# Linear-attention and ReGLU block on one core: PSUM banks by least recent use, split load queues, stages interleaved across phases

## The chip, the cores and the metric

The kernel runs on one core of a Trainium2 chip. The metric is device time in microseconds (us) of one execution. Single executions of one kernel mostly agree within 0.3%. A profile is one execution; its span (first to last instruction) is about 1.7 us shorter than its time.

Engines: PE is TensorE, DVE is VectorE, ACT is ScalarE, POOL is GpSimd, SP issues most loads and stores. PSUM is the memory that matmuls write to: 8 banks of 128 x 512 float32.

## The reference, cut to what matters

One token block of S = 2048 rows, D = 1024, F = 3584, 32 heads of 32, all bfloat16:

```python
h  = x + linear_attention(layernorm(x), wqkv, wo)   # phi(t) = where(t > 0, t + 1, exp(t)) + 1e-6
h2 = h + W_down( relu(LN(h) @ W_gate) * (LN(h) @ W_up) )
# attention per head: kv = phi(k)^T v ; z = sum phi(k) ; o = phi(q) kv / (phi(q) z + 1e-6)
```

A "tile" below is 128 rows; there are 16. The stages are: projections of k and v (KV, 64 groups of 8 matmuls), q (Q, 32 groups), phi(k)^T v (KVACC), then per tile numerator and denominator (ND), output projection with residual (A) and the second layer norm (LN2), then the feed-forward part: gate/up (GU) and down (DN) in four chunks of 512 rows.

## The kernel before

A small Python scheduler records each engine's instructions in the order of the program text. Each engine runs its own list strictly in that order; waits on semaphores are derived from buffers. This is the middle stage:

```python
for i in range(NT + 3):
    if i < NT:
        ND(i)                                   # PE: 8 matmuls into banks 5,6,7
                                                # DVE: 3 denominators, reciprocal, 3 multiplies -> otile
    if 0 <= i - 1 < NT:
        transpose_tile(otile ... i - 1)         # PE 8 transposes, ACT evacuates
    if 0 <= i - 2 < NT:
        A(i - 2, 0); A(i - 2, 1)                # PE 2 x 8 matmuls, DVE adds the residual into xh
        LN2(i - 2)                              # DVE bn_stats x2, aggregate, eps; POOL pow; DVE; ACT normalises
    if 0 <= i - 3 < NT:
        transpose_tile(ln2tile ... i - 3)       # PE, ACT
```

All 32 Q groups come before this loop and all GU groups after it. At the start, the loads of x and of the weights alternate on one queue; tile after tile is normalised on DVE, transposed, and multiplied with all four 512-column blocks of the k and v weights:

```python
load_x(0, 1); load_wkv(0); load_x(1, 1); load_wkv(1); ...
LN1(0); LN1(1); transpose 0; transpose 1
for t in range(NT):
    LN1(t + 2)
    for j in range(4): KV(t, j)
    transpose(t + 2)
```

Of the kernel before, what the change touches and what calls it, by code (L numbers as in the profile page):

```python
# [9 lines left out]
P = 128  # L10
# [11 lines left out]
class Buf:  # L22
    __slots__ = ("name", "writers", "readers", "exclusive")

    def __init__(self, name, exclusive=False):
        self.name = name
        self.writers = []
        self.readers = []
        self.exclusive = exclusive

# [30 lines left out]
class Sched:  # L61
# [38 lines left out]
    def _deps(self, eng, reads, writes, extra):  # L100
        deps = list(extra)
        semnum = eng.sem.num if eng.sem is not None else -1
        for b in reads:
            deps += b.deps_for_read(semnum)
        for b in writes:
            deps += b.deps_for_write()
        return deps
# [74 lines left out]
def bass_sequential_preLN__linear_attn_block__glu_gated_reglu__prompt_kernel(  # L182
# [21 lines left out]
    NS = 5  # L204
    NDB = (NG + 2) // 3
    EPS_LN = 1e-5

# [12 lines left out]
    WQ = al(PK + NT * D)  # L220
    SLOTS = X0
    slot_sz = al(KT * FPS * P)
    firstpart = max(WQ + KT * D - X0, NS * 2 * slot_sz)
    VEXT = al(X0 + firstpart)
    OT = VEXT
    vext_sz = NT * NG * 129
    Y0 = al(VEXT + max(vext_sz, KT * S))
    LN1TILES = Y0
    OTILES = Y0
    PHITMP = al(Y0 + 2 * D)  # L230
    LN2TILES = PHITMP
    CONSTS = al(PHITMP + max(4 * 512, 2 * D))
# [3 lines left out]
    WO = al(MASK4 + 4)  # L236
    KVZ = al(WO + KT * D)
    END1 = al(KVZ + NG * 132)
    WD = al(X0 + NS * 2 * slot_sz)
# [5 lines left out]
    with ExitStack() as es:  # L245
# [10 lines left out]
        stats2 = sbf("stats2", [P, NT, DC, 6])  # L256
        mv2 = sbf("mv2", [P, NT, 2])
# [34 lines left out]
        oT = view(OT, KT * S).rearrange("p (k s) -> p k s", k=KT)  # L292
        ln1tile = [view(LN1TILES + i * D, D) for i in range(2)]
        otile = [view(OTILES + i * D, D) for i in range(2)]
        etmp = [view(PHITMP + i * 512, 512) for i in range(2)]
        ttmp = [view(PHITMP + (2 + i) * 512, 512) for i in range(2)]
        ln2tile = [view(LN2TILES + i * D, D) for i in range(2)]
# [15 lines left out]

        b_x = [[Buf(f"x{t}_{n}") for n in range(DC)] for t in range(NT)]
        b_ln1T = [Buf(f"ln1T{t}") for t in range(NT)]
        b_ln2T = [Buf(f"ln2T{t}") for t in range(NT)]
        b_wkv = [Buf(f"wkv{j}") for j in range(2 * DC)]
        b_wq = [Buf(f"wq{j}") for j in range(DC)]
# [5 lines left out]
        b_hh = [Buf(f"hh{f}") for f in range(FT)]  # L324
        b_slot_g = [Buf(f"slotg{i}") for i in range(NS)]
        b_slot_u = [Buf(f"slotu{i}") for i in range(NS)]
        b_oT = [Buf(f"oT{t}") for t in range(NT)]
        b_ln1tile = [Buf(f"ln1tile{i}") for i in range(2)]
        b_otile = [Buf(f"otile{i}") for i in range(2)]
        b_etmp = [Buf(f"etmp{i}") for i in range(2)]  # L330
        b_ttmp = [Buf(f"ttmp{i}") for i in range(2)]
        b_ln2tile = [Buf(f"ln2tile{i}") for i in range(2)]
# [3 lines left out]
        b_kvz = [Buf(f"kvz{g}") for g in range(NG)]  # L336
        b_wd = [Buf(f"wd{i}") for i in range(4)]
        b_relu = [Buf(f"relu{i}") for i in range(2)]
        b_stage = [Buf(f"stage{i}") for i in range(4)]
        b_ps = [Buf(f"psum{i}", exclusive=True) for i in range(8)]  # L340
        b_stats1 = [Buf(f"stats1_{t}") for t in range(NT)]
        b_mv1 = [Buf(f"mv1_{t}") for t in range(NT)]
        b_veps1 = [Buf(f"veps1_{t}") for t in range(NT)]
        b_rstd1 = [Buf(f"rstd1_{t}") for t in range(NT)]
        b_stats2 = [Buf(f"stats2_{t}") for t in range(NT)]
        b_mv2 = [Buf(f"mv2_{t}") for t in range(NT)]
        b_veps2 = [Buf(f"veps2_{t}") for t in range(NT)]
        b_rstd2 = [Buf(f"rstd2_{t}") for t in range(NT)]
        b_nmr2 = [Buf(f"nmr2_{t}") for t in range(NT)]
        b_mhalf = Buf("mhalf")  # L350
        b_deneps = [Buf(f"deneps{i}") for i in range(2)]
        b_rden = [Buf(f"rden{i}") for i in range(2)]

        E = Sd.emit

        E("pool", lambda e: e.memset(ident, 1.0), writes=[b_ident])
        E("pool", lambda e: e.affine_select(ident, ident, pattern=[[-1, P]], compare_op=ALU.is_equal, fill=0.0,
                                            base=0, channel_multiplier=1), reads=[b_ident], writes=[b_ident])
        E("pool", lambda e: e.memset(mhalf[:], -0.5), writes=[b_mhalf])
# [7 lines left out]
        def load_x(t0, m):  # L367
            s_ = dsem()
            src = x2[t0 * P:(t0 + m) * P, :].rearrange("(t p) d -> p t d", p=P)
            Sd.dma("sp", lambda e: e.dma_start(xh[:, t0:t0 + m, :], src), s_,  # L370
                   writes=[b for t in range(t0, t0 + m) for b in b_x[t]])

        def load_wkv(j):
            s_ = dsem()
            src = A_wqkv[:, D + j * 512:D + (j + 1) * 512].rearrange("(k p) n -> p k n", p=P)
            Sd.dma("sp", lambda e: e.dma_start(wkv[:, :, j * 512:(j + 1) * 512], src), s_, writes=[b_wkv[j]])

        def load_wq(j):
            s_ = dsem()
            src = A_wqkv[:, j * 512:(j + 1) * 512].rearrange("(k p) n -> p k n", p=P)  # L380
            Sd.dma("sp", lambda e: e.dma_start(wq[:, :, j * 512:(j + 1) * 512], src), s_, writes=[b_wq[j]])

        def load_wo():
            s_ = dsem()
            src = A_wo.rearrange("(k p) n -> p k n", p=P)
            Sd.dma("sp", lambda e: e.dma_start(wo, src), s_, writes=[b_wo])

        load_x(0, 1)
        load_wkv(0)
        if NT > 1:  # L390
            load_x(1, 1)
        load_wkv(1)
        t0 = 2
        while t0 < NT:
# [3 lines left out]
            if t0 == 4:  # L398
                for j in range(2, 2 * DC):
                    load_wkv(j)  # L400
        if NT <= 4:
            for j in range(2, 2 * DC):
                load_wkv(j)
        for j in range(DC):
            load_wq(j)
        load_wo()

        psT_ring = Ring([0, 1])
        acc_ring = Ring([2, 3, 4, 5, 6, 7])
        phi_ring = Ring([0, 1])  # L410

        def LN_stats(t, stats, mv, veps, rstd, bs, bm, bv, br):
            for i in range(DC):
                E("dve", lambda e, i=i: e.bn_stats(stats[:, t, i, :], xh[:, t, i * 512:(i + 1) * 512]),  # L414
                  reads=[b_x[t][i]], writes=[bs[t]])
            E("dve", lambda e: e.bn_aggr(mv[:, t, :], stats[:, t].rearrange("p a b -> p (a b)")),
              reads=[bs[t]], writes=[bm[t]])
            E("dve", lambda e: e.tensor_scalar(veps[:, t:t + 1], mv[:, t, 1:2], EPS_LN, None, op0=ALU.add),
              reads=[bm[t]], writes=[bv[t]])
            E("pool", lambda e: e.tensor_tensor(rstd[:, t:t + 1], veps[:, t:t + 1], mhalf[:], op=ALU.pow),  # L420
              reads=[bv[t], b_mhalf], writes=[br[t]])

        def LN1(t):
            LN_stats(t, stats1, mv1, veps1, rstd1, b_stats1, b_mv1, b_veps1, b_rstd1)
            r = t % 2
            E("dve", lambda e: e.tensor_scalar(ln1tile[r], xh[:, t, :], mv1[:, t, 0:1], rstd1[:, t:t + 1],
                                               op0=ALU.subtract, op1=ALU.mult),
              reads=b_x[t] + [b_mv1[t], b_rstd1[t]], writes=[b_ln1tile[r]])

        def LN2(t):  # L430
            LN_stats(t, stats2, mv2, veps2, rstd2, b_stats2, b_mv2, b_veps2, b_rstd2)
            r = t % 2
            E("dve", lambda e: e.tensor_scalar(nmr2[:, t:t + 1], mv2[:, t, 0:1], rstd2[:, t:t + 1], -1.0,
                                               op0=ALU.mult, op1=ALU.mult),
              reads=[b_mv2[t], b_rstd2[t]], writes=[b_nmr2[t]])
            E("act", lambda e: e.activation(ln2tile[r], xh[:, t, :], ACT.Identity, bias=nmr2[:, t:t + 1],
                                            scale=rstd2[:, t:t + 1]),
              reads=b_x[t] + [b_nmr2[t], b_rstd2[t]], writes=[b_ln2tile[r]])

        def transpose_tile(src_ap, src_buf, dstT, dst_buf, t):  # L440
            bk = psT_ring.next()
            for k in range(KT):
                E("pe", lambda e, k=k: e.transpose(psum_bf[bk][:, k * P:(k + 1) * P], src_ap[:, k * P:(k + 1) * P], ident),  # L443
                  reads=[src_buf, b_ident], writes=[b_ps[bk]], inc=(k == KT - 1))
            E("act", lambda e: e.activation(dstT[:, :, t * P:(t + 1) * P],  # L445
                                            psum_bf[bk][:, 0:KT * P].rearrange("p (k s) -> p k s", k=KT), ACT.Copy),
              reads=[b_ps[bk]], writes=[dst_buf])
# [9 lines left out]
        def KV(t, j):  # L457
            bk = acc_ring.next()
# [12 lines left out]
        def KVACC(g):  # L471
            bk = acc_ring.next()
# [10 lines left out]
        def Q(f, c):  # L483
            bk = acc_ring.next()
# [7 lines left out]
        nd_banks = [5, 6, 7][:NDB]  # L492

        def ND(t):
            c = t // 4
            for g in range(NG):
                bk = nd_banks[g // 3]
# [4 lines left out]
            r = t % 2  # L502
            groups = [(i, list(range(3 * i, min(3 * i + 3, NG)))) for i in range(NDB)]
            for i, gs in groups:
                bk = nd_banks[i]
# [4 lines left out]
                E("dve", lambda e, src=src, dst=dst: e.tensor_scalar(dst, src, 1e-6, None, op0=ALU.add),  # L510
                  reads=[b_ps[bk]], writes=[b_deneps[r]])
            E("dve", lambda e: e.reciprocal(rden[:, r, :], deneps[:, r, :]), reads=[b_deneps[r]], writes=[b_rden[r]])  # L512
            for i, gs in groups:
                bk = nd_banks[i]
# [6 lines left out]
                dst = otile[r][:, g0 * P:(g0 + ng) * P].rearrange("p (g h e) -> p g h e", g=ng, h=4)  # L521
                E("dve", lambda e, src=src, rd=rd, dst=dst: e.tensor_tensor(dst, src, rd, op=ALU.mult),  # L522
                  reads=[b_ps[bk], b_rden[r]], writes=[b_otile[r]])

        a_ring = Ring([2, 3, 4])

        def A(t, n):
            bk = a_ring.next()
# [187 lines left out]
```

## Time and profile before

| | before |
|---|---|
| time, median of 13 runs | 891.3 us (890.79 to 892.34) |
| PE / DVE / ACT / POOL busy | 849.4 / 314.6 / 189.7 / 18.9 us |
| first KV matmul | 11.2 us |
| first Q, ND, GU, DN matmul | 129.7, 192.3, 303.7, 402.6 us |

The stage starts are the first starts of each matmul group. This is the view by stretches of the kernel before (start:end, length, then busy us and instructions of each engine, granted PE clock, share of DMA, GB/s):

```profile
0.00:11.20 11.20, 1.83 (x16) 1.57 (x17) 5.09 (x20) 2.31 (x2) 2.44 (x10) 1.00 0.87 291
11.20:130.00 118.80, 118.80 (x629) 57.03 (x627) 75.24 (x134) 51.59 (x79) 7.70 (x14) 1.00 0.23 79
...
192.40:300.00 107.60, 82.88 (x633) 46.42 (x630) 87.65 (x224) 46.77 (x46) 8.24 (x15) 0.97 0.20 50
```

PE is busy all the time in the projections, hardly at all in the first 11.2 us, and not enough in the middle. The first 32 projection matmuls take 8.58 us in the chain of waits and every later 32 take 6.91: the first ones run at half pace. PE is called cold below where its matmuls run at half pace, and warm at full pace. (The granted-clock column reads 0.50 in the next such stretch, 303.6 to 307.3 us, but 1.00 in this one; so in the first microseconds of a profile the pace of the matmuls decides.) A dense 512-column matmul costs 0.216 us (224 of them take 48.35 us in the chain of waits), so the middle's PE work is about 77 us of its 111 us. What binds there is told by the chain of waits. One tile of it (start, length, what; lines with only 0.02 us of "issue" are left out):

```profile
230.34 1.20 DVE big L533 x2
231.54 0.61 DVE stats L414
...
232.17 0.70 DVE stats L414
...
232.90 0.22 DVE mv L416
...
233.38 0.56 POOL rstd L420
...
233.96 0.21 DVE nmr L433
234.17 0.09 DVE deneps L510
...
234.69 0.36 DVE rden L512
...
235.08 0.57 DVE big L522
...
236.68 1.20 DVE big L533 x2
```

L533 is the residual add, L414 bn_stats, L510 the denominators, L512 the reciprocal, L522 the multiplies. From one add to the next is 6.34 us, nearly all of it DVE, with one hop over POOL.

### The profile page before, as it was taken

How to read it: one execution, taken by the hardware profiler on the slowest of the kernel's cores; microseconds unless marked ns; L12 is line 12 of the kernel's file. 1: busy time of each engine (PE TensorE's matmuls, PEld its weight loads, DVE VectorE, ACT ScalarE, POOL GpSimd, SP SyncE). 2: the span in 40 equal slices, each digit the busy share in tenths (PEclk: the TensorE clock that was granted, in tenths of full speed). 3: DMA queues.
4: the chain of work that ended last, by engine and by line, in shares of the span. 5: the costliest groups of instructions: out<-in, count | busy, mean ns of one | idle time of the engine just before them, and what ended most of it. 6: DMA issues, size and time to landing. Idle time of an engine off the chain costs nothing.

```text
span 889.2 us, 10230 instructions
## 1 busy us (share of the span) xinstructions
PE 849.4 (96%) x4352; PEld 401.5 (45%) x4352; DVE 314.6 (35%) x602; ACT 189.7 (21%) x273; POOL 18.9 (2%) x40
## 2 busy tenths in 40 slices
PE   5999999988787799999999999999999999999998
PEld 2444446444444344444444444444444444444443
DVE  5666647787888312121011211011121111122101
ACT  2444432323545411110011111001111001111100
POOL 1000000000000000000000000000000000000000
PEclk9999999989999899999999999999999999999999
DMA  9600000036000297552025555005555202551000
GB/s 329 238 1 1 1 1 2 0 84 153 1 1 1 92 347 198 152 158 60 24 85 162 144 144 145 21 24 142 147 161 158 68 24 74 155 161 49 1 24 24
DMA packets 134252, 83.49 MB, mean 94 GB/s; under 512 B 2624, under 2 KB 127552, under 8 KB 134208
## 3 DMA queue, kind: packets, MB, share of 16 engines
q1 hardware_dynamic: 134208, 82.85, 31.8%
q8 instruction: 34, 0.56, 0.3%
q14 instruction: 10, 0.08, 0.0%
HBM read 78.64 MB, written 4.19 MB: 93 GB/s over the span
## 4 chain that ended last, share of the span: by engine, by line
PE 87%; DVE 9%; issue 1%; POOL 1%; DMA 1%; ACT 0%; SPq 0%; POOLq 0%
PE ps L631 22%; PE ps L635 22%; PE ps L647 22%; PE ps L460 13%; PE ps L486 6%; DVE big L522 3%; DVE stats L414 2%; DVE big L533 2%; PE ps L443 1%; POOL rstd L420 1%; PE ps L530 1%; PE ps L475 1%; DVE deneps L510 1%; DMA big<-in_A_x_dram 1%; DVE rden L512 1%
## 5 line engine op out<-in xcount | busy, mean ns | idle before, releaser
L631 PE MATMUL ps<-big 128*128 128x512 bf16 x896 | 213.3, 381 | 0.0
L635 PE MATMUL ps<-big 128*128 128x512 bf16 x896 | 212.2, 380 | 0.0
L647 PE MATMUL ps<-big 128*128 128x512 bf16 x896 | 194.0, 379 | 0.0
L640 DVE TENSOR_TENSOR big<-ps,big 128x512 bf16<-128x512 f32 x112 | 77.5, 692 | 314.8 <-PE ps L635 314.8
L639 ACT ACTIVATE big<-ps 128x512 bf16<-128x512 f32 x112 | 66.9, 597 | 465.1 <-PE ps L631 465.1
L631 PEld LDWEIGHTS ps<-big 128*128 128x128 bf16 x896 | 87.9, 98 | 106.6 <-issue 1.9
L635 PEld LDWEIGHTS ps<-big 128*128 128x128 bf16 x896 | 87.9, 98 | 106.5 <-issue 1.3
L647 PEld LDWEIGHTS ps<-big 128*128 128x128 bf16 x896 | 87.7, 98 | 105.7
L460 PE MATMUL ps<-big 128*128 128x512 bf16 x512 | 114.7, 383 | 0.0
L651 DVE TENSOR_TENSOR big<-ps,big 128x512 bf16<-128x512 f32 x32 | 22.1, 692 | 171.3 <-PE ps L647 171.3
L460 PEld LDWEIGHTS ps<-big 128*128 128x128 bf16 x512 | 50.0, 99 | 58.1 <-issue 2.2
L443 PE MATMUL ps<-big 128*128 128x128 bf16 x384 | 31.6, 229 | 32.3 <-ACT big L445 18.0
L452 DVE TENSOR_SCALAR big<-ps 128x512 bf16<-128x512 f32 x64 | 44.3, 692 | 44.6 <-ACT big L451 44.6
L530 PE MATMUL ps<-big 128*128 128x512 bf16 x256 | 58.5, 382 | 0.3 <-ACT big L445 0.3
L486 PE MATMUL ps<-big 128*128 128x512 bf16 x256 | 55.6, 379 | 0.0
L451 ACT ACTIVATE big<-ps 128x512 bf16<-128x512 f32 x64 | 38.2, 597 | 74.3 <-PE ps L486 43.5
L445 ACT ACTIVATE big<-ps 128x1024 bf16<-128x1024 bf16 x48 | 47.3, 1012 | 16.0 <-PE ps L443 16.0
L414 DVE BATCH_NORM_STATS2 stats<-big 128x6 f32<-128x512 bf16 x64 | 44.1, 689 | 5.0 <-DMA big<-in_A_x_dram 3.9
L454 DVE SCALAR_TENSOR_TENSOR big<-big 128x512 bf16<-128x512 bf16 x64 | 44.3, 692 | 2.2
L443 PEld LDWEIGHTS ps<-big 128*128 128x128 bf16 x384 | 24.7, 102 | 43.3 <-ACT big L445 24.4
L486 PEld LDWEIGHTS ps<-big 128*128 128x128 bf16 x256 | 25.0, 98 | 30.0
L530 PEld LDWEIGHTS ps<-big 128*128 128x128 bf16 x256 | 24.6, 99 | 27.3 <-issue 0.8
(30 smaller groups left out, 182.3 us busy)
## 6 DMA issues: line engine op xcount, KB each, us to landing
big<-in_B_W_gate_dram SPq DMA_DIRECT2D x56, 512.0 KB, 3.9
big<-in_B_W_up_dram SPq DMA_DIRECT2D x56, 512.0 KB, 4.8
big<-in_B_W_down_dram SPq DMA_DIRECT2D x4, 1792.0 KB, 14.5
big<-in_A_wqkv_dram SPq DMA_DIRECT2D x6, 1024.0 KB, 11.6
out_dram<-big SPq DMA_DIRECT2D x32, 128.0 KB, 1.7
big<-in_A_x_dram SPq DMA_DIRECT2D x7, 512.0 KB, 9.6
big<-in_A_wo_dram SPq DMA_DIRECT2D x1, 2048.0 KB, 16.5
big<-in_A_x_dram SPq DMA_DIRECT2D x2, 256.0 KB, 4.2
```

The source lines that it names most:

```text
L414: E("dve", lambda e, i=i: e.bn_stats(stats[:, t, i, :], xh[:, t, i * 512:(i + 1) * 512]), reads=[b_x[t][i]], writes=[bs[t]])
L443: E("pe", lambda e, k=k: e.transpose(psum_bf[bk][:, k * P:(k + 1) * P], src_ap[:, k * P:(k + 1) * P], ident), reads=[src_buf, b_ident], wr ...
L445: E("act", lambda e: e.activation(dstT[:, :, t * P:(t + 1) * P], psum_bf[bk][:, 0:KT * P].rearrange("p (k s) -> p k s", k=KT), ACT.Copy), ...
L452: E("dve", lambda e: e.tensor_scalar(ttmp[r], psum[bk][:], 0.0, 1e-6, op0=ALU.max, op1=ALU.add), reads=[b_ps[bk]], writes=[b_ttmp[r]])
L460: E("pe", lambda e, k=k: e.matmul(psum[bk][:], lhsT=lnT[:, k, t * P:(t + 1) * P], rhs=wkv[:, k, j * 512:(j + 1) * 512], start=(k == 0), st ...
L486: E("pe", lambda e, k=k: e.matmul(psum[bk][:], lhsT=wq[:, k, f * P:(f + 1) * P], rhs=lnT[:, k, c * 512:(c + 1) * 512], start=(k == 0), sto ...
L530: E("pe", lambda e, k=k: e.matmul(psum[bk][:], lhsT=oT[:, k, t * P:(t + 1) * P], rhs=wo[:, k, n * 512:(n + 1) * 512], start=(k == 0), stop ...
L631: E("pe", lambda e, k=k: e.matmul(psum[gb][:], lhsT=wgs[slot][:, k, fo:fo + P], rhs=lnT[:, k, c * 512:(c + 1) * 512], start=(k == 0), stop ...
L635: E("pe", lambda e, k=k: e.matmul(psum[ub][:], lhsT=wus[slot][:, k, fo:fo + P], rhs=lnT[:, k, c * 512:(c + 1) * 512], start=(k == 0), stop ...
L639: E("act", lambda e: e.activation(relu[r], psum[gb][:], ACT.Relu), reads=[b_ps[gb]], writes=[b_relu[r]])
L640: E("dve", lambda e: e.tensor_tensor(hhT[:, f, :], psum[ub][:], relu[r], op=ALU.mult), reads=[b_ps[ub], b_relu[r]], writes=[b_hh[f]])
L647: E("pe", lambda e, f=f: e.matmul(psum[bk][:], lhsT=hhT[:, f, tt * P:(tt + 1) * P], rhs=wd[:, f, n * 512:(n + 1) * 512], start=(f == 0), s ...
```

## The change: intent and diff

The intent is to give PE work in every stage and to unload DVE:

1. PSUM banks are taken by least recent use over all eight, in place of fixed sets for each use.
2. LN2's sums come from the residual add's accumulator and from an ACT Square with accumulator; POOL normalises. The denominators go to ACT. In the first layer norm POOL normalises all but two tiles.
3. Half of the Q groups move into the first eight middle tiles (two per tile), and ten GU groups into its drain.
4. The start loads tile 0 in halves on two queues, issues dummy matmuls to warm PE, and works block by block (one weight block for four tiles) in place of tile by tile.
5. Weight slots of the feed-forward part go from 5 to 4, to make room. The tiles between stages (otile, ln2tile) get three buffers in place of two, and LN2's transposes come one step later (TL_LAG = 4 in place of 3).

The core of the diff (cuts marked by ...):

```diff
+        def alloc_banks(n=1):
+            order = sorted(range(8), key=lambda b: bank_last[b])
+            got = order[:n]
...
-    NS = 5
+    NS = 4
...
-                E("dve", lambda e, src=src, dst=dst: e.tensor_scalar(dst, src, 1e-6, None, op0=ALU.add),
+                E("act", lambda e, src=src, dst=dst: e.activation(dst, src, ACT.Identity, bias=1e-6),
...
-            E("dve", lambda e: e.tensor_tensor(xh[...], psum[bk][:], xh[...], op=ALU.add),
+            E("dve", lambda e: e.scalar_tensor_tensor(xs, psum[bk][:], 1.0, xs, op0=ALU.mult, op1=ALU.add,
+                                                      accum_out=sum2[:, t, n:n + 1]),
...
+        def LN2(t):
+            E("act", lambda e: e.activation(ln2tile[r], xh[:, t, :], ACT.Square, accum_out=sumsq2[:, t:t + 1]), ...
+            ... # DVE: mean2, t12, veps2 (one column each); POOL: rstd2, nmr2
+            E("pool", lambda e: e.tensor_scalar(ln2tile[r], xh[:, t, :], rstd2[:, t:t + 1], nmr2[:, t:t + 1], ...
...
+        LN1(blk0[0], True)
+        T1(blk0[0], "dve")
+        for idx, t in enumerate(blk0):
+            LN1(blk0[idx + 1], idx + 1 < 2)
+            KV(t, jorder[0])
+            T1(blk0[idx + 1])
...
+        for i in range(n_iter):
+            if i < NT:
+                ND(i)
+            ... # two Q groups while i < 8
+            if 0 <= i - 1 < NT:
+                TO(i - 1)
+            if 0 <= i - 2 < NT:
+                A(i - 2, 0); A(i - 2, 1); LN2(i - 2)
+            ... # two GU groups of chunk 0 when i >= NT
+            if 0 <= i - TL_LAG < NT:            # TL_LAG = 4
+                TL(i - TL_LAG)
```

## The prediction

> **What bounds the kernel now.** TensorE (PE) in every stage but three. By the busy-by-stretch view: projections (11.2 to 192.4 us) and the feed-forward part (about 311 to 886 us) are dense; one 512-column matmul costs 0.216 us start to start (224 take 48.35 us in the chain). PE does not bind in:
> 1. the first 11.2 us (PE busy 1.8), and then 1.7 us of cold clock (first 32 projection matmuls 8.58 us, later 6.91);
> 2. the middle, 192.4 to 303.7 us: 111 us for about 77 us of PE work (256 output matmuls 55.3, transposes 14.1, numerator matmuls 7.3). The chain there is DVE alone, 6.34 us per tile (229.92 to 236.26): output add 1.2, bn_stats 1.3, small statistics with a POOL hop 1.3, denominators 0.5, reciprocal 0.4, multiplies 1.6;
> 3. its drain, 288 to 303.7, and a cold feed-forward start (about 2.5 us).
>
> **What the change does.**
> - Per tile it takes bn_stats and aggregate (1.6 us) and the denominators off DVE; ACT gets Square and the denominators, POOL the normalisation. Square over 1024: estimate 1.04 us plus an accumulator read (the Trainium skill, "ScalarE: Activation LUTs", section What ACT_TABLE_LOAD costs: 186 ns + 0.833 ns per element; its form with two pointer operands gives 1.23 us, the trace has 1.24). POOL normalisation: estimate 0.9 to 2.2 us (the Trainium skill, "GPSIMD Engine Reference", section 3.1: 1.03 to 2.6 cycles per element); not binding.
> - 16 of 32 Q groups (27.6 us of PE) move into the first 8 middle tiles; 10 gate/up groups (34.5 us) into the drain.
> - The start normalises one tile at a time, with warm-up matmuls.
> - Weight slots go from 5 to 4.
>
> **Middle after.** DVE work falls to 4.2 us a tile, PE needs 4.95, but the queues are in order, which makes a serial ACT–DVE loop: output adds of tile i-2 → Square (1.2) → transpose evacuation (0.95) → three denominators of tile i+1 (0.6) → reciprocal (0.4) → multiplies (1.6) → adds of tile i-1 (1.5). About 6.3 us a tile, no better than now. Two Q groups put 2.8 us of phi on DVE into it: 9.05 us (PE 8.4). Hence ramp 17 us, five tiles 43 us, the last eight 50 us: 110 us, with 27.6 us of Q in it. The drain becomes dense PE: 43.7 us, 34.5 of it feed-forward.
>
> **Start.** The first projection begins near 8.6 us, but the next three tiles pass statistics, POOL, transpose and evacuation in series (4 us each): the same work ends 1 to 3 us later.
>
> **Down weights.** Their 7.3 MB go ahead of slot fills; four slots last 27.6 us against about 29: 1 us of stall.
>
> **Sum.** Middle and drain -20 to -22 us, start +1.5 to +2.5, stall +1: 891.75 → **872 us** (2.2% less), range 858 to 882. Chances: faster by over 2% 0.55, within 2% 0.42, slower 0.03.
>
> **What would show it.** The chain in the middle alternates ACT (Square, evacuation, denominators) with DVE; period near 9 us, then 6.3; PE 80% busy in the last eight tiles. Drain at full PE; no cold feed-forward start; one short wait on a gate slot. POOL busy up by 50 to 90 us, DVE down by 25.
>
> **What would make it wrong.** If ACT overlaps DVE better, PE binds (856). If POOL holds DVE up, or accumulator reads cost over 0.2 us, the loop lengthens (880). If PE stays cold over the thin first row, +4.

## The result, and the profile after

| | before | after |
|---|---|---|
| time, median | 891.3 us (13 runs) | 865.15 us (8 runs, 863.89 to 867.24) |
| PE / DVE / ACT / POOL busy | 849.4 / 314.6 / 189.7 / 18.9 us | 848.0 / 278.9 / 193.6 / 63.0 us |
| first KV matmul | 11.2 us | 9.7 us |
| first Q, ND, GU, DN matmul | 129.7, 192.3, 303.7, 402.6 us | 132.6, 167.5, 275.0, 377.0 us |

The ratio of the times is 0.9705 (95% interval 0.9695 to 0.9714): 2.95% faster.

Read the stage starts as differences. From start to Q the changed kernel is 2.9 us later. From the first Q to the first ND it takes 34.9 us in place of 62.6: 27.7 us less, for the 16 Q groups that moved out (16 x 8 x 0.216 = 27.6 us). From the first ND to the first DN it takes 209.5 us in place of 210.3, and now contains those 27.6 us. From DN on both take 486.6 us. So the gain of 25.6 us in the spans is 27.7 + 0.8 - 2.9: PE's waiting time in the middle and its drain has been filled with Q and GU work, and a little was lost at the start.

The stretches after (same columns as before), of which 167.65:232.00 are the tiles with Q and 232.00:270.00 the ones without:

```profile
0.00:9.70 9.70, 5.07 (x18) 1.79 (x18) 5.15 (x20) 1.49 (x2) 2.48 (x11) 1.00 0.74 248
9.70:23.60 13.90, 10.39 (x57) 4.86 (x57) 7.26 (x17) 4.53 (x6) 8.41 (x13) 0.88 1.08 368
...
167.65:232.00 64.35, 64.18 (x439) 34.80 (x436) 51.81 (x119) 31.85 (x69) 12.06 (x18) 1.00 0.00 1
232.00:270.00 38.00, 34.78 (x259) 18.90 (x257) 23.25 (x69) 23.28 (x49) 14.00 (x21) 1.00 0.01 1
```

In the last stretch no engine but PE is over 62% busy (ACT 23.28 of 38.00), and PE shows 92%. The chain of waits of the same stretch, one tile (L580 residual add with its accumulator, L586 Square, L483 transpose evacuation, L552 denominators, L554 reciprocal, L564 multiplies):

```profile
236.04 1.23 DVE big L580 x4
...
237.29 1.15 ACT big L586 x2
238.44 0.91 ACT big L483
239.35 0.08 ACT deneps L552
...
239.45 0.19 ACT deneps L552
...
239.66 0.19 ACT deneps L552
...
239.87 0.37 DVE rden L554
...
240.26 0.57 DVE big L564
240.83 0.02 issue
240.85 0.57 DVE big L564
...
241.44 0.42 DVE big L564
241.87 1.23 DVE big L580 x4
```

The reader should see that no piece of this chain is PE work, that it closes on itself after 5.83 us, and that it alternates between two engines, each of which waits for the other. The loop comes from the order of the two lists. ACT has the Square of tile i-2 ahead of the denominators of tile i+1, so these wait for the adds of tile i-2; DVE has the multiplies of tile i+1, which need the denominators, ahead of the adds of tile i-1. The chain of a tile with Q groups is the same with phi (L494, L496) between multiplies and adds, and closes after 8.48 us (207.41 to 215.89).

An instruction with an accumulator shows as two, the second being the read. Of the groups from 160 to 320 us (busy us, mean ns):

```profile
L580 DVE SCALAR_TENSOR_TENSOR big<-ps,big 128x512 bf16<-128x512 f32 x32 | 21.0, 684 | 3.7 <-PE ps L576 3.6
...
L586 ACT ACTIVATE big<-big 128x1024 bf16<-128x1024 bf16 x16 | 16.9, 1057 | 42.9 <-DVE big L580 42.9
...
L586 ACT ACTIVATION_READ_ACCUMULATOR big<-big 128x1 f32 x16 | 3.0, 187 | 0.0
...
L580 DVE DVE_READ_ACCUMULATOR big<-ps,big 128x1 f32 x32 | 2.6, 82 | 0.0
```

The drain, in PE's order of time: output projections (L576), then gate and up (L722, L726) without an idle gap:

```profile
271.53 3.62 PE L576 MATMUL ps<-big 128*128 128x512 bf16 x16
274.99 1.89 PE L722 MATMUL ps<-big 128*128 128x512 bf16 x8
276.71 1.89 PE L726 MATMUL ps<-big 128*128 128x512 bf16 x8
```

The start, in the chain of waits after:

```profile
1.68 7.92 DMA big<-in_A_wqkv_dram
...
9.74 3.53 PE ps L502 x8
...
14.85 1.91 PE ps L502 x8
18.36 1.92 PE ps L502 x8
21.86 8.81 PE ps L502 x40
```

The first projection waits for the first weight block and then runs at half speed (3.53 us against 1.91 for the same 8 matmuls; the granted clock is 0.50 from 10 to 12 us); each of the next tiles comes 3.5 us after the one before, of which 1.9 us is projection.

### The profile page after: what moved, and what is told of

Read it like the earlier page. It is cut to its first block, busy times and chain, and to the rows that moved or that the text cites. A ratio compares the mean times of both kernels' runs of the same rounds, so it can differ in the third digit from the quotient of the medians.

```text
span 863.6 us, 10334 instructions
## 1 busy us (share of the span) xinstructions
PE 848.0 (98%) x4362; PEld 400.9 (46%) x4362; DVE 278.9 (32%) x541; ACT 193.6 (22%) x337; POOL 63.0 (7%) x101
## 4 chain that ended last, share of the span: by engine, by line
PE 90%; DVE 5%; ACT 4%; DMA 1%; issue 0%; SPq 0%
PE ps L722 22%; PE ps L740 22%; PE ps L726 22%; PE ps L502 13%; PE ps L528 5%; PE ps L576 2%; DVE big L564 2%; DVE big L580 2%; ACT big L483 1%; ACT big L586 1%; PE ps L475 1%; DMA big<-in_A_wqkv_dram 1%; PE ps L517 1%; ACT deneps L552 1%; DVE big L496 0%; DVE rden L554 0%
## 5 line engine op out<-in xcount | busy, mean ns | idle before, releaser
L722 PE MATMUL ps<-big 128*128 128x512 bf16 x896 | 211.7, 379 | 0.0
L726 PE MATMUL ps<-big 128*128 128x512 bf16 x896 | 211.7, 379 | 0.0
L730 ACT ACTIVATE big<-ps 128x512 bf16<-128x512 f32 x112 | 66.8, 597 | 452.8 <-PE ps L722 452.8
L726 PEld LDWEIGHTS ps<-big 128*128 128x128 bf16 x896 | 87.7, 98 | 105.7 <-DMA big<-in_B_W_up_dram 0.3
L722 PEld LDWEIGHTS ps<-big 128*128 128x128 bf16 x896 | 87.5, 98 | 105.2 <-DMA big<-in_B_W_gate_dram 0.4
L494 DVE TENSOR_SCALAR big<-ps 128x512 bf16<-128x512 f32 x64 | 44.1, 689 | 59.3 <-ACT big L493 59.3
L576 PE MATMUL ps<-big 128*128 128x512 bf16 x256 | 57.9, 379 | 0.0
L528 PE MATMUL ps<-big 128*128 128x512 bf16 x256 | 56.9, 379 | 0.0
L493 ACT ACTIVATE big<-ps 128x512 bf16<-128x512 f32 x64 | 38.2, 597 | 68.5 <-PE ps L528 34.7
L483 ACT ACTIVATE big<-ps 128x1024 bf16<-128x1024 bf16 x47 | 47.5, 1014 | 6.3 <-PE ps L475 6.3
L496 DVE SCALAR_TENSOR_TENSOR big<-big 128x512 bf16<-128x512 bf16 x64 | 44.3, 692 | 2.2
L576 PEld LDWEIGHTS ps<-big 128*128 128x128 bf16 x256 | 24.4, 98 | 26.4
L475 PE MATMUL ps<-big 128*128 128x128 bf16 x384 | 29.2, 219 | 2.5 <-DVE big L564 2.5
L509 ACT ACTIVATE big<-ps 128x512 bf16<-128x512 f32 x32 | 19.2, 600 | 45.3 <-PE ps L502 45.3
## 6 DMA issues: line engine op xcount, KB each, us to landing
big<-in_A_x_dram SPq DMA_DIRECT2D x6, 512.0 KB, 10.6
```

Source lines behind the costliest of these rows:

```text
L475: E("pe", lambda e, k=k: e.transpose(psum_bf[bk][:, k * P:(k + 1) * P], src_ap[:, k * P:(k + 1) * P], ident), reads=[src_buf, b_ident], wr ...
L483: E("act", lambda e: e.activation(dst, src, ACT.Copy), reads=[b_ps[bk]], writes=[dst_buf])
L494: E("dve", lambda e: e.tensor_scalar(ttmp[r], psum[bk][:], 0.0, 1e-6, op0=ALU.max, op1=ALU.add), reads=[b_ps[bk]], writes=[b_ttmp[r]])
L496: E("dve", lambda e: e.scalar_tensor_tensor(dst_ap, etmp[r], 1.0, ttmp[r], op0=ALU.min, op1=ALU.add), reads=[b_etmp[r], b_ttmp[r]], writes ...
L528: E("pe", lambda e, k=k: e.matmul(psum[bk][:], lhsT=wq[:, k, f * P:(f + 1) * P], rhs=lnT[:, k, c * 512:(c + 1) * 512], start=(k == 0), sto ...
L576: E("pe", lambda e, k=k: e.matmul(psum[bk][:], lhsT=oT[:, k, ts_ * P:(ts_ + 1) * P], rhs=wo[:, k, n * 512:(n + 1) * 512], start=(k == 0), ...
```

## The experiments

Eleven kernels ran, all gave correct results. In the diffs `...` marks cuts, and text in parentheses or after # stands for code left out. The kernel before measured 891.2 to 891.4 us beside each set. Times are medians (4 runs each) and differences are to the changed kernel's 865.15 us.

| run | what | us | difference |
|---|---|---|---|
| e1_order | LN2 issued after the next tile's ND | 856.61 | -8.5 |
| e2_sq2 | Square done twice | 880.25 | +15.1 |
| e3_order_sq2 | both | 855.65 | -9.5 |
| e4_no_gu | no GU in the drain | 870.30 | +5.2 |
| e5_q_early | all Q before the middle | 872.40 | +7.3 |
| e6_old_ln2 | LN2 and denominators as before | 875.76 | +10.6 |
| e7_old_start | start as before | 862.50 | -2.7 |
| e8_old_banks | fixed PSUM banks | 868.61 | +3.5 |
| e11_w_first | first weight block loaded ahead of tile 1 | 863.58 | -1.6 |
| e9_best | e1 and an improved old start | 854.73 | -10.4 |
| e10_pairs | e1 and a start in pairs of tiles | 853.09 | -12.1 |

### Is the middle bound by a loop of issue order, or by an engine?

Theory: the serial ACT-DVE loop of the prediction. Rivals: DVE throughput, POOL holding DVE up, or PSUM banks. Three runs, two edits crossed.

The edit of e1_order moves one call; nothing is added or removed. ACT's list then has the Square of tile i-3, whose adds were issued one step earlier, ahead of the denominators of tile i+1:

```diff
     if i < NT:
         ND(i)
+    if 0 <= i - 3 < NT:
+        LN2(i - 3)
...
         A(i - 2, 0); A(i - 2, 1)
-        LN2(i - 2)
```

> Only the place of the second layer norm in the issue order moves: it is issued after the next tile's numerator step instead of before it. No instruction is added or taken away. Serial-loop theory (adds of tile i-2, Square, transpose evacuation, denominators of tile i+1, reciprocal, multiplies, adds of tile i-1): the loop then spans two tiles and stops binding; the last eight tiles fall from 5.83 us to TensorE's 4.95 us each, the Q tiles from 8.48 to about 8.35; in all 6 to 8 us, about 858 us. Rivals (VectorE throughput, POOL holding VectorE up, PSUM banks): work, port use and banks are the same, so the period stays 5.8 us and the time 865.

Measured: 856.61 us (ratio 0.961 to the kernel before). The summary of the chain of waits from 170 to 290 us has no DVE and no ACT in it any more:

```profile
by line: PE ps L576 45.5%; PE ps L528 22.1%; PE ps L475 11.2%; PE ps L722 7.9%; PE ps L726 7.2%; PE ps L540 5.8%; issue 0.7%
```

In the order of time of PE, output projections now begin 4.81 us apart (L576):

```profile
226.00 3.62 PE L576 MATMUL ps<-big 128*128 128x512 bf16 x15
...
230.81 3.62 PE L576 MATMUL ps<-big 128*128 128x512 bf16 x16
```

The edit of e2_sq2 issues the same Square a second time:

```diff
             E("act", lambda e: e.activation(ln2tile[r], xh[:, t, :], ACT.Square, accum_out=sumsq2[:, t:t + 1]), ...
+            E("act", lambda e: e.activation(ln2tile[r], xh[:, t, :], ACT.Square, accum_out=sumsq2[:, t:t + 1]), ...
```

> The changed kernel with every Square of the second layer norm issued twice (same result), 1.15 us more ScalarE work per tile. ScalarE is only 61% busy in the last eight tiles. Serial-loop theory: every one of these microseconds enters the period: 5.83 to about 6.98 us in the last eight tiles, 8.48 to 9.6 in the Q tiles that the loop binds, +11 to +15 us in all, about 878. Rivals (VectorE, POOL or PSUM bound, ScalarE with slack): less than +3 us.

Measured: 880.25 us, +15.1 us, just over what was expected. The added Square is in the chain of every tile, and the period from add to add is 7.02 us in the last eight tiles (it was 5.83) and 9.67 in a Q tile (209.40 to 219.07; it was 8.48):

```profile
235.75 1.23 DVE big L580 x4
...
237.00 1.16 ACT big L586 x2
...
238.19 1.15 ACT big L588 x2
239.34 0.91 ACT big L483
...
242.77 1.23 DVE big L580 x4
```

e3_order_sq2 has both edits.

> Reordered as in e1_order, and the Square doubled as in e2_sq2. Serial-loop theory: with the loop opened the same extra 1.15 us per tile falls into ScalarE's slack (about 4.7 of 4.95 us busy): 0 to +2 us over e1_order. If doubling costs +11 us here as well, ScalarE's throughput and not the loop was the matter.

Measured: 855.65 us, 0.96 us below e1_order, with ranges that overlap (855.11 to 857.76, and 855.53 to 857.79). Output projections are again 4.8 us apart:

```profile
253.00 3.62 PE L576 MATMUL ps<-big 128*128 128x512 bf16 x15
...
257.82 3.62 PE L576 MATMUL ps<-big 128*128 128x512 bf16 x16
```

The two profiles differ in the start alone: from the first Q to the end it is 722.9 us in e1_order and 722.8 in e3_order_sq2. So doubling the Square costs nothing when the loop is open, and 15 us when it is closed. ACT's throughput was never the matter. Together the three runs show that the order in the two queues bound the middle; the rivals need no part in it. Nor does POOL slow DVE's multiplies: three groups take 557 ns in the kernel before, where POOL does not normalise, and 557 ns in the changed kernel.

### What did each part of the change bring?

Each of these undoes one part in the changed kernel. The parts overlap, so their costs need not add up to the gain.

e4_no_gu switches off the GU groups in the drain:

```diff
-            if i >= NT and gi < len(gu_tasks) and gu_tasks[gi][0] == 0:
+            if False and gi < len(gu_tasks) and gu_tasks[gi][0] == 0:
```

> The changed kernel without the ten gate/up groups in the drain of the middle (they come after it). In the changed kernel the drain lasts 43.9 us (271.1 to 315.0), of which 34.5 us are these groups, so 9.4 us for what must be done there. Theory (the groups fill time in which TensorE would wait for the last two tiles' layer norm): the bare drain takes 13 to 15 us, and the feed-forward part may begin cold; +4 to +6 us, about 870. If the drain could be dense anyway: +0.

Measured: 870.30 us. PE's order of time shows the bare drain from 269.66 (last otile transpose) to 282.92 us (first GU), 13.3 us, a wait of 3.3 us for POOL's last normalisation, and a cold first GU:

```profile
277.47 1.35 PE L475 MATMUL ps<-big 128*128 128x128 bf16 x16
282.10 1.03 PE L475 MATMUL ps<-big 128*128 128x128 bf16 x8 [3.28 <-POOL big L607]
282.92 3.62 PE L722 MATMUL ps<-big 128*128 128x512 bf16 x8
```

e5_q_early takes all Q groups before the middle:

```diff
-        n_pre = min(len(q_tasks), 2 * KT) if NCH > 2 else len(q_tasks)
+        n_pre = len(q_tasks)
```

> The changed kernel with all 32 Q groups before the middle, as in the kernel before (27.6 us of dense TensorE work moves back out of the first eight tiles). Theory: all sixteen tiles then run at the loop's 5.83 us, and the ramp is bare: +6 to +8 us, about 872. If the gain of the change came from elsewhere: under +2.

Measured: 872.40 us. From the third tile on all tiles run at the loop's 5.83 us (adds at 215.28, 221.11, 226.94 and so on). The Q groups gain because a Q tile takes 8.48 us, against 5.83 us for the loop alone plus 3.45 us for two Q groups issued elsewhere.

e6_old_ln2 puts back bn_stats, DVE's denominators and ACT's normalisation, in the new schedule:

```diff
-                E("act", ... e.activation(dst, src, ACT.Identity, bias=1e-6)
+                E("dve", ... e.tensor_scalar(dst, src, 1e-6, None, op0=ALU.add)
...
-            (ACT Square with accumulator, DVE columns, POOL normalises)
+            (DVE bn_stats x2, bn_aggr, eps; POOL pow; DVE; ACT normalises)
```

> The changed kernel's schedule with the second layer norm and the denominators of the kernel before: bn_stats and the denominators on VectorE, normalisation on ScalarE. Theory: the period is VectorE's 6.3 us in the last eight tiles (now 5.83) and about 9.1 in the Q tiles (now 8.48, or TensorE's 8.35): +5 to +9 us, about 872. It tells what moving work off VectorE brought by itself.

Measured: 875.76 us, a little more than expected. Here DVE's list is the loop: the period is 6.35 us in the last tiles (one nmr to the next, 238.96 to 245.31) as in the kernel before, and 9.29 us in a Q tile. So moving the statistics, the normalisation and the denominators was worth 10.6 us, although it left the period only 0.5 to 0.8 us shorter. The two profiles tell where it went. From the first ND to the adds of the third tile e6 takes 35.7 us in place of 31.1 (in the changed kernel these tiles run at PE's pace), which is 4.6 us; the next three tiles take 2.2 us more, and the eight after them 4.1.

e8_old_banks replaces the least-recently-used choice by the fixed sets of the kernel before:

```diff
-            bk = alloc_banks(1)[0]      # everywhere
+            bk = ring.next()            # transposes 0,1; KV, KVACC, early Q 2..7; A and middle Q 2..4; DN 4..7
-            banks = alloc_banks(NDB)
+            banks = [5, 6, 7]           # ND
-            gb, ub = alloc_banks(2)
+            gb, ub = ring_gu.next()     # (0,1), (2,3)
```

> The changed kernel with fixed PSUM banks by use as in the kernel before (transposes 0-1, numerators 5-7, output and middle Q groups 2-4, gate/up in pairs 0-3, down 4-7) in place of the least-recently-used choice over all eight. Theory (bank waits do not bind; the ACT-VectorE loop does): 0 to +3 us, at most 868. If the bank choice was what freed the schedule: +6 us or more.

Measured: 868.61 us (867.2 to 871.79), slightly over the range. Compared by stages, because the start differs between profiles: the middle's sixteen tiles are unchanged (from its first ND to its first GU 107.5 us in both). ND's fixed banks wait 1.42 us for a phi of the last Q group, and from the first GU to the first DN it takes 104.0 us in place of 102.0:

```profile
167.43 0.64 PE L548 MATMUL ps<-big 128*128 128x132 bf16 x8 [1.42 <-DVE big L501]
```

So the bank choice gives about 3.5 us at the two joints, where uses that shared no bank before come to overlap, and nothing inside a stage.

e7_old_start puts back the load order and the tile-by-tile start, without warm-up matmuls:

```diff
-        (tile 0 in halves on two queues; tile 1; weight block; ... ; 10 dummy matmuls; rows of one weight block)
+        load_x(0, 1); load_wkv(0, "sp"); load_x(1, 1); load_wkv(1, "sp"); ...
+        LN1(0, True); LN1(1, True); T1(0); T1(1)
+        for t in range(NT):
+            LN1(t + 2, True)
+            for j in range(2 * DC):
+                KV(t, j)
+            T1(t + 2)
```

> The changed kernel with the start of the kernel before: its load order, all first layer norms normalised on VectorE, tile after tile with all four weight blocks, no warm-up matmuls, no load on the ScalarE queue. In the changed kernel the projections end at 132.7 us, before at 129.9. Theory (the new start costs time, because the first row serves one tile at a time and the first weight block lands at 9.6 us): 2 to 3.5 us faster than the changed kernel, about 862. Rival (the new start gains, and something else pushed the projections back): slower, 866 to 868.

Measured: 862.50 us (861.99 to 862.92), 2.65 us faster than the changed kernel. Its projections end at 129.5 us, like those of the kernel before. The new start is a loss, as predicted, inside a change that gains.

### What sets the start, and the wider spread of times?

The changed kernel's eight times span 3.4 us, and those of the kernel before 1.6. In the profiles of runs with the new start the first projection began at 9.7, 10.4, 8.5, 8.5, 8.6, 9.1, 7.7 and 8.1 us (after, e1 to e6, e8; e7 has the old start). In all eight that is about 0.14 us after the first weight block landed, which took 5.9 to 8.5 us from its issue.

```diff
         load_x(0, 1, halves=True)
-        if NT > 1:
-            load_x(1, 1)
         load_wkv(jorder[0], "sp")
+        if NT > 1:
+            load_x(1, 1)
```

> The changed kernel with one line moved: the load of the first weight block is issued right after tile 0 of x, ahead of tile 1. In the profiles so far the first projection of this start began anywhere from 7.7 to 10.4 us, waiting for that block up to 3.2 us[...]; times spread over 3.4 us (863.9 to 867.2), the kernel before over 1.6. Theory (the landing of that block sets the start and its spread): the first projection begins near 7.5 to 8 us in every run, 0.5 to 2 us faster (about 864), spread under 2 us. Rival (tile 1 of x, now later, sets the first row): no gain or a loss.

Measured: 863.58 us, all four times within 863.51 to 863.85. The wait for the weight block is gone; the first projection began at 8.26 us, just behind the evacuation of its own transpose (0.79 us idle before it), a little later than expected. One exchanged line brought 1.6 us in the medians (the intervals of the two ratios just overlap, 0.9670 to 0.9699 and 0.9695 to 0.9714) and took the spread from 3.4 us (8 runs) to 0.34 (4 runs); the other runs with the new start spread over 2.2 to 4.6 us, e7 with the old start over 0.9. So the landing of the first weight block behind tile 1 was what scattered most of the times, as far as sets of four runs can show it.

### A version that beats both

e9_best joins e1_order with the old start, tile 1 loaded ahead of the weights, and 14 more dummy matmuls between the first two transposes:

```diff
+        load_x(0, 1, halves=True); load_x(1, 1); load_wkv(0, "sp"); load_wkv(1, "sp"); ...
+        LN1(0, True); LN1(1, True); T1(0)
+        (14 dummy matmuls)
+        T1(1)
+        (then as in e7_old_start)
```

> Second layer norm reordered as in e1_order, with the start of the kernel before (tile after tile, all four weight blocks), but tile 1 of x loaded ahead of the weights and dummy matmuls keeping TensorE warm until the first projection. Old start alone brought -2.65 us; a warm first row 1.7 us more, tile 1 earlier 0 to 1: 851 to 853 us.

Measured: 854.73 us, 1.7 us short of the expected range. PE is warm (8 matmuls in 1.90 us), but now it is too early for the weights: it waits twice for the later blocks, 0.75 and 1.10 us, and its projections end at 129.6 us, no earlier than with the old start alone (129.5).

e10_pairs joins e1_order with a start that asks for a new weight block only every second projection:

```diff
+        load_x(0, 1, halves=True); load_wkv(0, "sp"); load_x(1, 1); load_wkv(1, "sp"); load_x(2, 2); ...
...
+        LN1(0, True); T1(0, "dve")
+        (5 dummy matmuls)
+        LN1(1, True); KV(0, 0); T1(1)
+        for t in range(0, NT, 2):
+            for j in range(4):
+                (LN1 of tiles t+2, t+3 before j = 0 and 2)
+                KV(t, j); KV(t + 1, j)
+                (T1 of tiles t+2, t+3 after j = 1 and 3)
```

> Second layer norm reordered as in e1_order, and another start: first weight block ahead of tile 1, warm-up kept, projections in pairs of tiles (block 0 for both, then block 1 and so on), so that TensorE has two projections for every transpose and needs a new weight block only every 3.5 us. If the first block lands by 8.5 us and the next ones in time, the projections end near 127 us instead of 132.7: about 851 us. If TensorE then waits for weight blocks 1 to 3 instead (they land behind each other on the same engines), no better than e9_best.

Measured: 853.09 us (852.48 to 853.88), ratio 0.9567 to the kernel before: 4.3% faster than it, and 12.1 us faster than the changed kernel. It is 2 us short of the expected 851: the projections end at 129.1 us, not near 127. PE's order of time shows the first projection at 7.73 us, two idle gaps of about 1 us, and dense work after:

```profile
7.73 1.89 PE L491 MATMUL ps<-big 128*128 128x512 bf16 x8
10.59 0.62 PE L464 MATMUL ps<-big 128*128 128x128 bf16 x8 [0.97 <-DVE big L450]
12.33 7.04 PE L491 MATMUL ps<-big 128*128 128x512 bf16 x23 [1.12 <-ACT big L472]
```

## Why the prediction was right or wrong

The time was right: 872 us with a range of 858 to 882, measured 865.15; faster by over 2% had 0.55 and came true. Point by point:

- **The loop.** Right, and shown by e1 to e3: adds, Square, evacuation, denominators, reciprocal, multiplies, adds. Its size was too large: 6.3 us predicted, 5.83 measured, and 9.05 against 8.48 with Q. Term by term, predicted and measured: adds 1.5 and 1.23; Square 1.2 and 1.15; evacuation 0.95 and 0.91; denominators 0.6 and 0.50; reciprocal 0.4 and 0.37; multiplies 1.6 and 1.60. The worst term was the adds: the accumulator reads last 82 ns, but two adds still start only 0.61 us apart. The last eight tiles took 46.7 us, predicted 50, and the tiles before them 56.9, predicted 60: together 6.5 us, nearly the whole distance between 872 and 865. Of the other terms, the start (about 2 predicted, 2.9 measured) and the stall (1 and 0.1) were off in opposite directions and cancelled, which is luck.
- **"No better than now."** Slightly off for that reason: 5.83 against 6.34 us.
- **The drain.** Right: dense PE from 271.1 to about 315 us, no cold feed-forward start. Without the GU groups it is 13.3 us and cold (e4).
- **The start.** Right that it ends later: 2.9 us in the profile, predicted 1 to 3, and e7 confirms 2.65 us. The step "the first projection begins near 8.6 us" missed that it can wait for the first weight block (2.73 us in the profile) and can then be cold.
- **Down weights.** Predicted 1 us of stall with four slots. The chain shows one group of 8 matmuls at 1.80 us where its neighbours take 1.73, so about 0.1 us. The term was too large.
- **PE share.** "80% busy in the last eight tiles" shows as 92% in the view by stretches, but PE's own pace there is 4.81 us (e1), and 4.81 / 5.83 is 82%. The Trainium skill, page "Trainium Kernel Development and Optimization", section Performance Expectations, warns that matmul busy time is a bad metric because matmuls are pipelined; the trace agrees.
- **The two cited estimates.** Square: 186 + 0.833 x 1024 ns is 1.04 us by the skill's "ScalarE: Activation LUTs" (section What ACT_TABLE_LOAD costs); the trace has 1.06 us plus an accumulator read of 0.19 (1.15 for both in the chain, as they overlap). POOL's normalisation: 0.9 to 2.2 us by "GPSIMD Engine Reference" (section 3.1); the trace has 1.20. Both hold.
- **Busy times.** POOL rose by 44 us (predicted 50 to 90), DVE fell by 36 (predicted 25), ACT rose by 4. They are not what sets the time.

What stays open: what the third buffers, the later LN2 transposes and the four weight slots bring, which no run tests alone; and what decides whether PE is cold at the first projection. With all idle time after the warm-up matmuls counted, it was warm after 0.79, 1.24 and 1.28 us (e11, e4, e6) and cold after 1.89 to 3.23 (after, e1, e2, e3, e5, e8); no run varied this by itself. The warm-up itself varies: in these nine profiles the same ten dummy matmuls took from 3.62 us (e8) to 4.45. The skill's page "TensorE: Matmul & The Clock Gate" (Part 1) calls the window in which activity sets the clock free-running and the number of cold matmuls variable from run to run, which fits; no run here tests it.

## What to carry to other kernels

When work is spread over engines, compute for every pair of engines the loop that their in-order lists make, not only each engine's sum: here ACT and DVE, each busy 61% of the time, bound a stage that PE could have run in 4.81 us, and moving one call by one position was worth 8.5 us. Test such a loop by doubling one cheap link twice: with the loop as it is, and with an order that opens it. And look at parts of a large change one at a time: this one carried a start that cost 2.7 us, and a load order that scattered its times.

## What the Trainium skill lacked or had wrong

- "ScalarE: Activation LUTs": it mentions the accumulator output but not its cost. The runs show a separate instruction of 187 ns behind each Square, of which 0.09 us adds to the chain (1.15 us for both, 1.06 for the Square).
- "VectorE: DVE Perf Modes" (section Two Vector instructions with no wait between them): it says that an accumulating op is two instructions, without a time. The read took 82 ns, and two residual adds with their reads took 1.23 us in the chain, against 1.20 in the kernel before without them.
- "GPSIMD Engine Reference" (section 3): no figure for a bfloat16 tensor_scalar with two per-partition operands. 128 x 1024 took 1.20 us, the same op on one column 0.26 us, and a pow on one column 0.55 us.
- "DMA: Bandwidth & Descriptors": no page tells how much the landing of a transfer scatters when others are queued ahead of it. Here the first weight block, 1 MB behind 0.5 MB of x, landed 5.9 to 8.5 us after its issue and let the first projection start anywhere from 7.7 to 10.4 us; with 0.25 MB ahead of it, it landed in 5.5 us in the one profile taken (e11), and the four times agreed within 0.34 us.
